# A gated linear recurrence with a convolution gate: a new order of all operations, a third x buffer, one ring for gate and gated value, a shorter setup

## The chip, the cores and the metric

The kernel runs on one core of a Trainium2 chip. Times are device microseconds. The time of a kernel is the median over its runs; one more execution is recorded by the hardware profiler, and the profile, with all its times inside the kernel, is of that one.

## What is computed

Four sequences of 6,336 tokens with 256 channels, 25,344 tokens in all, in float32. Two layers, one after the other:

```python
a_base  = sigmoid(a_param)
log_a   = 8.0 * sigmoid(r_gate) * log(clip(a_base, 1e-6, 1 - 1e-6))
a_t     = exp(log_a)
x_gated = sqrt(max(1 - a_t * a_t, 1e-6)) * sigmoid(i_gate) * x
h       = a_t[:, t] * h + x_gated[:, t]        # for every t; y[:, t] = h
...
gate    = sigmoid(sum_k conv_w[k] * y[t - 4 + k])   # causal, 5 taps
out     = (gate * (y @ w_val)) @ w_out
```

## The kernel before

**Tiling.** The tokens are cut into 27 chunks: chunk 0 has 512 tokens, chunks 1 to 23 have 1,024, chunks 24 and 25 have 512, chunk 26 has 256. From the convolution on, a chunk is worked in parts of 512 tokens. Inputs arrive with tokens on the partitions. The recurrence needs channels on the partitions (two halves, h = 0 and 1), so values are transposed by TensorE on the way.

**One operation, one name.** The whole work is a list of named operations, `name.chunk.half_or_part.bank`, in the string PLAN. The last number is the PSUM bank, or -1. The kernel goes through the list and calls `op_<name>` for each entry. Each engine takes its own operations in the order of the list, so PLAN fixes the order on every engine; waits between engines follow from what is read and written. The names, with their engine and the line of the profile:

- `ldri`, `ldx`, `ldw` (SP): loads of r and i (two DMAs, L220), of x (L224), of the two weights (L229, L231). SP issues them in order, so a load whose buffer is not free holds up those behind it.
- `tanh` (ACT, L290): tanh of half of r and i at once, in place, as bf16. Sigmoid is made of tanh.
- `srT` (PE, L295): transposes the r half, then `exp` (ACT, L304): a_t into aring. `e` (POOL, L310): its square into ering.
- `s1` (POOL, L318): 1 + tanh of i, then `u` (POOL, L345): times x, into uring. For the chunks in X_PE (0 and 1) x goes through PE into PSUM instead (`xc`, L327) and DVE does both steps (`ux`, L335, four steps for a full chunk).
- `sq` (ACT, L354): half of sqrt(1 - a squared), for up to three chunks in one entry. Sqrt is in another table of ACT than tanh and exp, so a table load (L472) stands before and after.
- `nT` (PE, L367) transposes it back, `xg` (DVE, L374) multiplies it into u, `xgT` (PE, L382) transposes the product to channels, `scan` (DVE, L395) runs the recurrence into yring.
- `conv` (PE, L407) is the 5-tap convolution by diagonal weights, `tg` (ACT, L417) its tanh into tgr, `val` (PE, L425) is y times w_val, `gv` (DVE, L430) is (1 + tanh) times val into gvr, `out` (PE, L439) is the product with w_out.
- `osbD` (DVE, L454) or `osbA` (ACT, L450) copies a part to osb, `store` writes it from ACT's queue (L459).
- `wc` (ACT, L282 and L284): casts of the weights to bf16.

**Buffers.** Rings with a fixed number of places: NRI = 3 for the r and i pair, NX = 2 for x, NA = 5 for a, NE = 5 for e, NU = 4 for u, NY = 3 for y, NOSB = 5 for outputs, NTG = 2 for the gate's tanh and NGV = 2 for the gated value. The r place of a chunk is free after its `srT`, the i place and the x place after its `u`. So the i load of chunk c waits for `u` of chunk c - 3.

**Order around the middle.** ACT works in groups of three chunks: one `sq` for three, then three `tanh`, six `exp` and six `tg`. The setup ahead of the list loads a_param and conv_w from ACT's queue, computes the scale of the exponent, and builds the diagonal weights. Loads at the head of PLAN are issued before all else.

Of the kernel before, what the change touches and what calls it, by code (L numbers as in the profile page):

```python
# [8 lines left out]
P = 128  # L9
HP = 64  # L10
# [6 lines left out]
X_PE = [0, 1]  # L17
NRI = 3
NX = 2
NA = 5  # L20
NE = 5
NU = 4
NY = 3
NOSB = 5
NTG = 2
NGV = 2
# [7 lines left out]
ldri.0.-1 ldri.1.-1 ldx.0.-1 ldx.1.-1 ldri.2.-1 ldw.-1 tanh.0.-1 srT.0.0.7 srT.0.1.5 exp.0.1.-1 exp.0.0.-1 e.0.0.-1  # L34
tanh.1.-1 e.0.1.-1 xc.0.1.0 xc.0.0.6 ux.0.0.-1 xc.1.2.1 u.0.-1 sq.0.1.-1 ux.1.2.-1 srT.1.0.0 ldri.3.-1 xc.1.1.5
ldx.2.-1 nT.0.0.7 srT.1.1.4 exp.1.0.-1 xg.0.0.-1 ux.1.1.-1 exp.1.1.-1 xc.1.0.0 tanh.2.-1 xc.1.3.5 e.1.1.-1 ux.1.0.-1
e.1.0.-1 wc.-1 srT.2.0.3 s1.2.-1 srT.2.1.2 xgT.0.0.4 exp.2.0.-1 scan.0.0.-1 exp.2.1.-1 e.2.0.-1 u.1.-1 tanh.3.-1
ldx.3.-1 ldri.4.-1 e.2.1.-1 u.2.-1 srT.3.1.3 srT.3.0.6 xgT.0.1.1 sq.1.2.-1 s1.3.-1 ldx.4.-1 ldri.5.-1 nT.2.0.7
nT.2.1.0 u.3.-1 xg.2.0.-1 exp.3.1.-1 xg.2.1.-1 nT.1.1.7 scan.0.1.-1 nT.1.0.5 tanh.4.-1 xg.1.1.-1 conv.0.0.0 xg.1.0.-1
xgT.2.0.3 e.3.1.-1 ldx.5.-1 xgT.1.1.4 ldri.6.-1 xgT.1.0.2 scan.1.1.-1 tg.0.0.-1 exp.3.0.-1 s1.4.-1 srT.4.1.1  # L40
exp.4.1.-1 scan.1.0.-1 val.0.0.4 e.3.0.-1 tanh.5.-1 srT.4.0.6 gv.0.0.-1 conv.1.0.0 u.4.-1 scan.2.0.-1 xgT.2.1.7
tg.1.0.-1 srT.5.1.5 srT.5.0.4 exp.4.0.-1 scan.2.1.-1 val.1.0.0 exp.5.1.-1 e.4.1.-1 ldx.6.-1 ldri.7.-1 exp.5.0.-1
gv.1.0.-1 conv.2.0.6 tanh.6.-1 e.5.1.-1 out.0.0.4 conv.1.1.0 osbD.0.0.-1 e.4.0.-1 val.2.0.2 tg.1.1.-1 val.1.1.4
e.5.0.-1 store.0.0.-1 tg.2.0.-1 out.1.0.0 conv.2.1.6 osbD.1.0.-1 s1.5.-1 sq.3.3.-1 gv.1.1.-1 u.5.-1 gv.2.0.-1
out.2.0.0 out.1.1.4 osbD.2.0.-1 osbD.1.1.-1 s1.6.-1 nT.3.1.3 ldri.8.-1 nT.3.0.2 ldx.7.-1 val.2.1.0 tg.2.1.-1 xg.3.0.-1
xg.3.1.-1 store.1.0.-1 u.6.-1 tanh.7.-1 gv.2.1.-1 xgT.3.1.7 nT.4.0.6 scan.3.1.-1 srT.6.0.1 srT.6.1.4 xgT.3.0.2
nT.4.1.0 nT.5.1.5 exp.6.0.-1 xg.4.0.-1 s1.7.-1 ldri.9.-1 xg.4.1.-1 exp.6.1.-1 srT.7.0.1 xg.5.1.-1 ldx.8.-1 nT.5.0.6
scan.3.0.-1 exp.7.0.-1 out.2.1.4 e.6.1.-1 tanh.8.-1 xgT.4.1.3 srT.7.1.7 xg.5.0.-1 conv.3.0.0 e.7.0.-1 osbD.2.1.-1
scan.4.1.-1 conv.3.1.4 u.7.-1 store.1.1.-1 tg.3.0.-1 xgT.4.0.6 srT.8.0.2 tg.3.1.-1 scan.4.0.-1 srT.8.1.0 exp.7.1.-1
val.3.1.4 exp.8.1.-1 gv.3.1.-1 e.6.0.-1 conv.4.1.6 ldx.9.-1 exp.8.0.-1 ldri.10.-1 xgT.5.0.3 store.2.0.-1 tg.4.1.-1  # L50
out.3.1.4 e.7.1.-1 scan.5.0.-1 tanh.9.-1 xgT.5.1.7 val.3.0.0 e.8.0.-1 conv.4.0.2 gv.3.0.-1 osbD.3.1.-1 e.8.1.-1
tg.4.0.-1 scan.5.1.-1 val.4.1.4 s1.8.-1 val.4.0.0 sq.6.3.-1 out.3.0.2 gv.4.1.-1 u.8.-1 gv.4.0.-1 osbD.3.0.-1 out.4.0.0
out.4.1.2 osbD.4.0.-1 srT.9.1.6 osbD.4.1.-1 nT.8.1.5 s1.9.-1 ldri.11.-1 nT.6.1.4 xg.8.1.-1 exp.9.1.-1 conv.5.0.2
ldx.10.-1 xg.6.1.-1 store.3.0.-1 tanh.10.-1 e.9.1.-1 nT.6.0.4 nT.7.1.1 xg.6.0.-1 nT.7.0.0 xgT.6.1.5 xg.7.0.-1 u.9.-1
xgT.6.0.4 xg.7.1.-1 srT.9.0.6 scan.6.0.-1 nT.8.0.7 exp.9.0.-1 conv.5.1.0 tg.5.0.-1 scan.6.1.-1 tg.5.1.-1 xgT.7.1.2
s1.10.-1 ldri.12.-1 store.2.1.-1 tanh.11.-1 val.5.1.0 ldx.11.-1 xg.8.0.-1 srT.10.1.3 srT.10.0.6 gv.5.1.-1 e.9.0.-1
val.5.0.4 conv.6.1.0 gv.5.0.-1 exp.10.1.-1 u.10.-1 srT.11.1.7 scan.7.1.-1 store.3.1.-1 store.4.1.-1 conv.6.0.4
tg.6.1.-1 exp.10.0.-1 srT.11.0.1 xgT.7.0.0 tg.6.0.-1 val.6.0.2 scan.7.0.-1 exp.11.0.-1 e.10.0.-1 out.5.0.4 ldri.13.-1
store.4.0.-1 ldx.12.-1 exp.11.1.-1 osbD.5.0.-1 out.5.1.0 e.10.1.-1 tanh.12.-1 conv.7.0.6 osbD.5.1.-1 e.11.0.-1
val.6.1.4 gv.6.0.-1 gv.6.1.-1 out.6.0.2 tg.7.0.-1 e.11.1.-1 store.5.1.-1 osbD.6.0.-1 xgT.8.1.6 xgT.8.0.7 s1.11.-1  # L60
out.6.1.4 scan.8.1.-1 sq.9.3.-1 val.7.0.2 u.11.-1 gv.7.0.-1 osbD.6.1.-1 conv.7.1.2 scan.8.0.-1 srT.12.0.1 srT.12.1.6
nT.9.0.0 nT.9.1.4 s1.12.-1 ldri.14.-1 nT.11.0.5 xg.9.0.-1 exp.12.0.-1 nT.10.0.7 ldx.13.-1 xg.9.1.-1 store.6.1.-1
xg.11.0.-1 store.5.0.-1 tg.7.1.-1 xgT.9.1.0 e.12.0.-1 scan.9.1.-1 exp.12.1.-1 out.7.0.2 tanh.13.-1 val.7.1.4 u.12.-1
osbD.7.0.-1 conv.8.0.0 gv.7.1.-1 nT.10.1.2 xgT.9.0.3 xg.10.1.-1 tg.8.0.-1 srT.13.0.6 scan.9.0.-1 s1.13.-1 ldri.15.-1
# [442 lines left out]
```

## Time and profile before

| | us |
|---|---|
| median of 13 runs | 309.73 (308.91 to 311.59) |
| the profiled execution | 310.86 |
| its span, first to last instruction | 309.0 |
| mean granted TensorE clock | 0.967 |
| bytes read and written | 78.39 MB and 25.95 MB |

The table sets the profiled execution beside the runs: 1.86 us of its time lie around the span, and it is 1.13 above the median. Names in the profile: PE is TensorE, PEld its weight loads, DVE VectorE, ACT ScalarE, POOL GpSimd, SP the engine that issues the loads; ACTq and SPq are the queues from which DMAs are issued. A row of a timeline has start, duration, engine, line, operation and tiles, and in square brackets how long the engine had been idle before it and what ended that. In the chain of waits, the work that ended last is followed back; its largest parts by engine are PE 26%, DMA 19%, ACT 18%, DVE 14% and "issue" 11%. No engine has a majority.

Some durations of one instruction, from the groups by form: scan of 1,024 tokens 2,340 ns, u of a full chunk 4,117, e of one half 1,895, tanh of a full chunk 3,626, gv 1,213, output copy on DVE 1,214 and on ACT 1,010, table load 1,283.

### The profile page before, as it was taken

The page shows a single profiled execution, that of the slowest core. Times are in us where ns is not written, and L with a number is a line of the kernel's source. Part 1 is how long each engine was busy: PE and PEld are TensorE (multiplying, and loading weights), DVE is VectorE, ACT ScalarE, POOL GpSimd, SP SyncE. Part 2 cuts the span into 40 slices and gives each one's busy share as a digit, 9 for nine tenths or more (in the row PEclk, how much of TensorE's full clock was granted, in tenths as well). Part 3 has the DMA queues.
Part 4 walks back from the last instruction along what each step waited for, and adds up shares of the span by engine and source line. Part 5 has one row for each costly group of instructions (what it writes and reads, how often), then busy time and mean ns, then how long its engine had stood idle before and what let it go on. Part 6 is the DMA issues. An engine that isn't in the chain of part 4 may idle for free.

```text
span 309.0 us, 6335 instructions
## 1 busy us (share of the span) xinstructions
PE 247.6 (80%) x2627; PEld 167.3 (54%) x2627; DVE 252.1 (82%) x208; ACT 278.3 (90%) x185; POOL 235.0 (76%) x118
## 2 busy tenths in 40 slices
PE   0393387958887898799499998988899988899994
PEld 0242364537555665556257664675666656565763
DVE  1052079489998989999499999999999998989993
ACT  6699999999999999998599999999999989868632
POOL 2209999997998999899996799989959993038000
PEclk9996579999999999999979999999999999999999
DMA  7999899998996999999999997999898773183555
GB/s 288 423 354 423 327 423 372 408 361 314 381 405 223 407 415 424 423 421 423 427 422 379 371 375 291 383 424 418 329 368 313 285 260 138 68 329 116 202 211 237
DMA packets 19466, 104.74 MB, mean 339 GB/s; under 512 B 2151, under 2 KB 2670, under 8 KB 10606
## 3 DMA queue, kind: packets, MB, share of 16 engines
q1 hardware_dynamic: 12224, 78.39, 64.7%
q10 hardware_dynamic: 7214, 25.96, 21.0%
q8 instruction: 20, 0.33, 0.4%
q14 instruction: 8, 0.07, 0.1%
HBM read 78.39 MB, written 25.95 MB: 338 GB/s over the span
## 4 chain that ended last, share of the span: by engine, by line
PE 26%; DMA 19%; ACT 18%; DVE 14%; issue 11%; POOL 9%; ACTq 1%; SPq 1%; DVEq 0%; POOLq 0%
DMA gate<-in_i_gate_dram 10%; DVE yring L395 8%; PE pp L407 8%; DMA xr<-in_x_dram 6%; POOL uring L345 6%; PE pp L439 5%; ACT gate L290 5%; ACT tgr L417 4%; PE pp L425 4%; ACT aring L304 4%; PE pp L367 4%; DMA out_dram<-osb 3%; DVE osb L454 3%; DVE gvr L430 3%; ACT ering L354 2%
## 5 line engine op out<-in xcount | busy, mean ns | idle before, releaser
L310 POOL TENSOR_TENSOR ering<-aring 128x1024 f32<-128x1024 f32 (+2 forms) x54 | 93.6, 1752 | 37.0 <-ACT aring L304 36.8
L395 DVE TENSOR_TENSOR_SCAN yring<-aring,yring,pp 128x1024 bf16<-128x1024 f32 (+2 forms) x52 | 113.5, 2196 | 3.7 <-PE pp L382 3.6
L345 POOL TENSOR_TENSOR uring<-gate,xr 128x2048 bf16<-128x2048 bf16 (+2 forms) x25 | 96.0, 3842 | 4.4 <-PE pp L382 2.6
L290 ACT ACTIVATE gate<-gate 128x4096 bf16<-128x4096 f32 (+2 forms) x27 | 90.2, 3340 | 8.7 <-DMA gate<-in_i_gate_dram 4.5
L407 PE MATMUL pp<-yring,diag 64*64 64x512 bf16 (+13 forms) x1224 | 65.2, 341 | 6.2 <-DVE yring L395 2.7
L430 DVE SCALAR_TENSOR_TENSOR gvr<-tgr,pp 128x1024 bf16<-128x1024 bf16 (+1 forms) x50 | 59.5, 1202 | 8.7 <-ACT tgr L417 6.7
L439 PE MATMUL pp<-wo,gvr 128*128 128x256 bf16 x396 | 52.4, 278 | 13.7 <-DVE gvr L430 8.0
L304 ACT ACTIVATE aring<-pp,khf 128x1024 f32<-128x1024 bf16 (+2 forms) x54 | 59.2, 1141 | 2.8 <-PE pp L295 2.0
L417 ACT ACTIVATE tgr<-pp 128x1024 bf16<-128x1024 f32 (+1 forms) x50 | 50.4, 1022 | 10.1 <-PE pp L407 8.6
L439 PEld LDWEIGHTS <-gvr 128*128 128x128 bf16 x396 | 42.2, 115 | 23.4 <-DVE gvr L430 11.1
L425 PE MATMUL pp<-yring,wv 128*128 128x512 bf16 (+1 forms) x200 | 50.5, 377 | 5.3 <-DVE osb L454 1.9
L454 DVE COPY osb<-pp 128x1024 f32<-128x1024 f32 x41 | 49.1, 1214 | 5.9 <-PE pp L439 5.8
L318 POOL TENSOR_SCALAR gate<-gate 128x2048 bf16<-128x2048 bf16 (+2 forms) x25 | 44.4, 1779 | 5.4 <-ACT gate L290 5.4
L407 PEld LDWEIGHTS <-diag 64*64 64x64 bf16 x1224 | 30.4, 107 | 31.7 <-issue 15.0
L354 ACT ACTIVATE ering<-ering,b 128x4096 bf16<-128x4096 f32 (+4 forms) x16 | 46.4, 2932 | 0.1
L374 DVE TENSOR_TENSOR uring<-uring,pp 128x1024 bf16<-128x1024 bf16 (+1 forms) x50 | 32.1, 673 | 12.3 <-PE pp L367 12.1
L295 PE MATMUL pp<-ident_b,gate 128*128 128x128 bf16 x396 | 31.2, 229 | 12.8 <-ACT gate L290 10.7
L295 PEld LDWEIGHTS <-gate 128*128 128x128 bf16 x396 | 26.4, 103 | 21.4 <-ACT gate L290 13.3
L367 PE MATMUL pp<-ident_f,ering 128*128 128x128 f32 x198 | 32.3, 303 | 5.5 <-ACT ering L354 3.9
L382 PE MATMUL pp<-ident_f,uring 128*128 128x128 f32 x198 | 32.0, 285 | 5.2 <-ACT tgr L417 2.8
L367 PEld LDWEIGHTS pp<-ident_f,ering 128*128 128x128 f32 x198 | 27.8, 208 | 11.7 <-ACT ering L354 4.7
L425 PEld LDWEIGHTS <-wv 128*128 128x128 bf16 x200 | 18.9, 98 | 23.2 <-issue 10.4
(33 smaller groups left out, 87.2 us busy)
## 6 DMA issues: line engine op xcount, KB each, us to landing
out_dram<-osb ACTq DMA_DIRECT2D x49, 512.0 KB, 7.4
gate<-in_r_gate_dram SPq DMA_DIRECT2D x23, 1024.0 KB, 11.5
gate<-in_i_gate_dram SPq DMA_DIRECT2D x23, 1024.0 KB, 9.9
xr<-in_x_dram SPq DMA_DIRECT2D x23, 1024.0 KB, 9.7
gate<-in_r_gate_dram SPq DMA_DIRECT2D x3, 512.0 KB, 7.6
gate<-in_i_gate_dram SPq DMA_DIRECT2D x3, 512.0 KB, 10.9
xr<-in_x_dram SPq DMA_DIRECT2D x3, 512.0 KB, 3.4
yring<-in_moe_w_val_dram SPq DMA_DIRECT2D x1, 256.0 KB
```

The lines of the kernel that those rows point to most:

```text
L290: nc.scalar.activation(out=tgate[:, s0:s0 + 2, 0:w], in_=gate[:, s0:s0 + 2, 0:w], func=ACT.Tanh, scale=0.5)
L304: nc.scalar.activation(out=dst, in_=src, func=ACT.Exp, scale=khf[:, h:h + 1], bias=khf[:, h:h + 1])
L310: nc.gpsimd.tensor_tensor(out=ering[:, c % NE, h * n:(h + 1) * n], in0=a, in1=a, op=ALU.mult)
L345: nc.gpsimd.tensor_tensor(out=u, in0=t, in1=xt, op=ALU.mult)
L367: nc.tensor.transpose(out=pp[:, d0:d0 + P], in_=src[:, w, :], identity=ident_f[:])
L395: nc.vector.tensor_tensor_scan(out=yring[:, h, y0:y0 + n], data0=aring[:, c % NA, h, 0:n], data1=src, initial=prev, op0=ALU.mult, op1=ALU.add)
L407: nc.tensor.matmul(out=pp[col * HP:(col + 1) * HP, b0 + d0:b0 + d1], lhsT=diag[r * HP:(r + 1) * HP, h, kk, :], rhs=yring[r * HP:(r + 1) * ...
L417: nc.scalar.activation(out=tgr[:, nth[k] % NTG, :, 0:n], in_=two(live["conv", k], n), func=ACT.Tanh, scale=0.5)
L425: nc.tensor.matmul(out=pp[:, (bank + m) * BANK:(bank + m) * BANK + n], lhsT=wv[:, hk, m, :], rhs=yring[:, hk, y0:y0 + n], start=(hk == 0), ...
L430: nc.vector.scalar_tensor_tensor(out=gvr[:, nth[k] % NGV, :, 0:n], in0=tgr[:, nth[k] % NTG, :, 0:n], scalar=1.0, in1=two(live["val", k], n ...
L439: nc.tensor.matmul(out=pp[:, bank * BANK + j * D:bank * BANK + (j + 1) * D], lhsT=gvr[:, nth[k] % NGV, m, 0:n].rearrange("c (p q) -> c q p ...
L454: nc.vector.tensor_copy(out=dst, in_=src)
```

## The change

PLAN is a different list: the same operations in another order on every engine. Beside it:

- `X_PE` is empty, so x of chunks 0 and 1 no longer goes through PE: six `xc` and six `ux` steps go, two `s1` and two `u` on POOL come.
- `NX` is 3 (was 2), `NU` is 3 (was 4). `gvr` is gone: `gv` writes its result over the gate's tanh in `tgr`, and `NTG` is 3 (was 2).
- Chunk 0's r and i are two loads and two tanh (`ldr`, `ldi`, `tanh.0`, `tanhi.0`).
- The setup computes log(1 + exp(-a)) in one Ln with a bias of 1 and clips after it; add, reciprocal and clip before the Ln go. Small setup tiles lie in osb's last place. The load of conv_w is issued after the first table load.
- `wc` runs on POOL.
- In the list, x loads often follow the gate loads of two or three chunks together (for instance ldri.13, ldri.14, ldri.15, then ldx.13, ldx.14, ldx.15). Twelve output copies are on ACT (were nine), all in the last chunks.

The head of the old list and of the new one, then the rest of the diff, cut:

```diff
-ldri.0.-1 ldri.1.-1 ldx.0.-1 ldx.1.-1 ldri.2.-1 ldw.-1 tanh.0.-1 srT.0.0.7 srT.0.1.5 exp.0.1.-1 exp.0.0.-1 e.0.0.-1
-tanh.1.-1 e.0.1.-1 xc.0.1.0 xc.0.0.6 ux.0.0.-1 xc.1.2.1 u.0.-1 sq.0.1.-1 ux.1.2.-1 srT.1.0.0 ldri.3.-1 xc.1.1.5
+ldr.0.-1 ldi.0.-1 ldri.1.-1 ldx.0.-1 ldw.-1 ldri.2.-1 tanh.0.-1 ldx.1.-1 tanhi.0.-1 srT.0.1.1 srT.0.0.5 exp.0.0.-1
+exp.0.1.-1 e.0.0.-1 e.0.1.-1 s1.0.-1 sq.0.1.-1 nT.0.0.1 u.0.-1 tanh.1.-1 wc.-1 xg.0.0.-1 ldri.3.-1 xgT.0.1.1 ldx.3.-1
...
-X_PE = [0, 1]
+X_PE = []
 NRI = 3
-NX = 2
+NX = 3
 NA = 5
 NE = 5
-NU = 4
+NU = 3
 NY = 3
 NOSB = 5
-NTG = 2
-NGV = 2
+NTG = 3
...
-        ap2 = const.tile([H, P], FP32, name="ap2")
-        nc.scalar.dma_start(ap2[:], a_param.rearrange("(h p) -> h p", p=P))
-        wrow = const.tile([CONV_K, D], FP32, name="wrow")
-        nc.scalar.dma_start(wrow[:], moe_conv_w[:, :])
+        ap2 = osb[0:H, NOSB - 1, 0:P]
+        nc.scalar.dma_start(ap2, a_param.rearrange("(h p) -> h p", p=P))
...
         nc.scalar.preload_act_table_set("natural_log_exp_and_others")
+        wrow = osb[0:CONV_K, NOSB - 1, D:2 * D]
+        nc.scalar.dma_start(wrow, moe_conv_w[:, :])
...
-        ksig = const.tile([P, H], FP32, name="ksig")
-        nc.vector.tensor_scalar(out=ksig[:], in0=kex[:], scalar1=1.0, scalar2=None, op0=ALU.add)
-        nc.vector.reciprocal(out=ksig[:], in_=ksig[:])
-        nc.vector.tensor_scalar(out=ksig[:], in0=ksig[:], scalar1=1e-6, scalar2=1.0 - 1e-6,
-                                op0=ALU.max, op1=ALU.min)
-        nc.scalar.activation(out=kln[:], in_=ksig[:], func=ACT.Ln)
+        kln = const.tile([P, H], FP32, name="kln")
+        nc.scalar.activation(out=kln[:], in_=kex[:], func=ACT.Ln, bias=1.0)
...
-                nc.scalar.copy(out=wv[:, hk, :, :].rearrange("p m (i c) -> p i m c", i=2),
-                               in_=wvf[:, hk, :].rearrange("p (i m c) -> p i m c", i=2, m=2))
-            nc.scalar.activation(out=wo2[:], in_=wof, func=ACT.Copy, scale=0.5)
+                nc.gpsimd.tensor_scalar(out=wv[:, hk, :, :].rearrange("p m (i c) -> p i m c", i=2),
+                                        in0=wvf[:, hk, :].rearrange("p (i m c) -> p i m c", i=2, m=2),
+                                        scalar1=1.0, scalar2=1.0, op0=ALU.mult, op1=ALU.mult)
+            nc.gpsimd.tensor_scalar(out=wo2[:], in0=wof, scalar1=0.5, scalar2=1.0, op0=ALU.mult, op1=ALU.mult)
...
+            s0, s1 = slot(c, 0), slot(c, 0) + (1 if c == 0 else 2)
+            nc.scalar.activation(out=tgate[:, s0:s1, 0:w], in_=gate[:, s0:s1, 0:w], func=ACT.Tanh, scale=0.5)
...
-            nc.vector.scalar_tensor_tensor(out=gvr[:, nth[k] % NGV, :, 0:n], in0=tgr[:, nth[k] % NTG, :, 0:n], scalar=1.0,
+            nc.vector.scalar_tensor_tensor(out=tgr[:, nth[k] % NTG, :, 0:n], in0=tgr[:, nth[k] % NTG, :, 0:n], scalar=1.0,
                                            in1=two(live["val", k], n), op0=ALU.add, op1=ALU.mult)
...
-                                     lhsT=gvr[:, nth[k] % NGV, m, 0:n].rearrange("c (p q) -> c q p", q=q)[:, j, :],
+                                     lhsT=tgr[:, nth[k] % NTG, m, 0:n].rearrange("c (p q) -> c q p", q=q)[:, j, :],
```

From the old list, the order on SP between chunks 12 and 16 is ldri.12, ldx.11, ldri.13, ldx.12, ldri.14, ldx.13, ldri.15, ldx.14, ldx.15. On ACT the new order of the group from the sqrt of chunks 9 to 11 is sq.9.3, exp.12.0, exp.12.1, tg.7.1, tanh.13, tg.8.1, tg.8.0, exp.13.1, tanh.14, exp.13.0, tg.9.0, exp.14.0, exp.14.1, tanh.15, with stores between; on POOL it is e.11.0, u.10, s1.12, u.11, e.12.1, u.12, e.12.0, e.13.1, s1.13, e.13.0, e.14.0, e.14.1, u.13.

## The prediction

> **What bounds the kernel now.** I read the busy row of the page first, then busy time by stretch, then ScalarE's timeline, then the transfer rates.
>
> ```profile
> PE 247.6 (80%) x2627; PEld 167.3 (54%) x2627; DVE 252.1 (82%) x208; ACT 278.3 (90%) x185; POOL 235.0 (76%) x118
> ```
>
> The windows view gives, for each stretch, its length and the busy time of PE, PEld, DVE, ACT and POOL, then clock, DMA share and GB/s:
>
> ```profile
> 0.00:20.00 20.00, 8.27 (x27) 4.14 (x28) 3.20 (x10) 14.10 (x12) 4.35 (x10) 1.00 0.92 362
> 20.00:100.00 80.00, 57.47 (x572) 39.62 (x571) 55.92 (x46) 79.07 (x48) 73.84 (x34) 0.89 0.93 361
> 100.00:140.00 40.00, 34.30 (x391) 23.73 (x391) 38.41 (x30) 39.90 (x24) 38.86 (x19) 1.00 1.01 418
> 140.00:150.00 10.00, 9.27 (x111) 6.03 (x109) 9.35 (x7) 5.98 (x6) 10.00 (x5) 1.00 1.02 425
> 150.00:246.15 96.15, 84.11 (x911) 58.31 (x912) 91.03 (x73) 95.74 (x58) 86.09 (x38) 0.98 0.93 367
> 246.15:309.00 62.85, 54.17 (x622) 35.47 (x620) 54.15 (x45) 43.49 (x40) 21.87 (x15) 1.00 0.52 197
> ```
>
> ACT is full from 20 to 140 and from 150 to 246. It idles in three places: 5.9 us in the first 20, 4.0 in 140:150, 19.4 in the last 62.85, where PE (54.2) and DVE (54.2) are the fuller engines. So a new order can win in the opening, in that one hole and in the tail; in between it can only lose.
>
> ACT's period for three full chunks, from start-to-start distances in its timeline (tanh 3.51, exp 1.10, gate tanh 0.91, sqrt of three chunks 5.44, table load 1.30): 3x3.51 + 6x1.10 + 6x0.91 + 5.44 + 2x1.30 = 30.6 us (154.58 to 185.30 measures 30.7). The same chunks move 3 x 4 MiB = 12.58 MB.
>
> ```profile
> GB/s 288 423 354 423 327 423 372 408 361 314 381 405 223 407 415 424 423 421 423 427 422 379 371 375 291 383 424 418 329 368 313 285 260 138 68 329 116 202 211 237
> ```
>
> No slice passes 427; a row of slices stands at 421 to 424 with loads and stores mixed, so I take 424 GB/s: 29.7 us a group, 0.9 below ACT. **Here a rule of the skill differs.** The Trainium skill, "DMA: Bandwidth & Descriptors", section "Where 436 GB/s comes from", says that between HBM and SBUF a limit of about 358 GB/s binds. By it a group would take 35.1 us, transfers would be the bound throughout, and no order could help. The row holds 424 for over 50 us, so the row decides; but transfers are only 3% from binding.
>
> **The hole.** Up to 146.8 the slices sum to 55.7 MB, 131.5 us at 424: 15.3 us of transfer time had been lost before. It came due here:
>
> ```profile
> 150.03 3.62 ACT L290 ACTIVATE gate<-gate 128x4096 bf16<-128x4096 f32 x1 [4.05 <-DMA xr<-in_x_dram]
> ```
>
> (tanh of chunk 15; its own i load was in the same queue.)
>
> **Part 1, the opening.**
>
> ```profile
> 12.14 3.62 ACT L290 ACTIVATE gate<-gate 128x4096 bf16<-128x4096 f32 x1 [1.96 <-DMA gate<-in_i_gate_dram]
> 15.77 1.28 ACT L472 ACT_TABLE_LOAD   x1
> 17.07 1.15 ACT L354 ACTIVATE ering<-ering,b 128x1024 bf16<-128x1024 f32 x1
> 18.24 1.28 ACT L472 ACT_TABLE_LOAD   x1
> 19.53 1.21 ACT L304 ACTIVATE aring<-pp,khf 128x1024 f32<-128x1024 bf16 x1
> ...
> 25.75 0.70 ACT L282 CAST wv<-yring 128x256 bf16<-128x256 f32 x2
> 26.35 0.63 ACT L284 ACTIVATE wo<-yring 128x512 bf16<-128x512 f32 x1
> ```
>
> Before, sqrt of chunk 0 and its two table loads follow tanh 1 (3.76 us); now they precede it, in the wait for the i load. Walk: three small DVE steps between Exp and Ln go (3.07 to 3.71), so the second table load ends near 4.6 instead of 5.2. The two split tanh (1.06 each, row of the 128x1024 form) run 4.6 to 6.7. The conv_w load is issued later; it took 3.2 us (1.31 to about 4.5), and PE's first srT stands behind its transposes: exp by about 8.8, POOL's squares by 10.1, sqrt and tables by 12.5. Tanh 1 starts at 12.5, not 12.1, since its loads keep their place: the setup alone wins nothing, the data hides it. Tanh 1 ends near 16.0.
>
> Then a new wait. PE's srT.1.1 stands behind xgT.0.1, which needs u.0, now on POOL (2.15 us) and needing x 0 (landed 13.3 before): u.0 15.5, xg 16.2, srT 17.0; exp of chunk 1 17.1 to 19.4, tanh 2 to 22.9, gate tanh 0 and exp of chunk 2 to 26.0, tanh 3 to 29.5, table 30.8. In the old order the same work, without that gate tanh, ends at 34.09.
>
> The weight casts leave ACT (1.3 us) and join POOL. Nearest rows: 1,024 columns at the rate of L318 (1.90 for 2,048) are 1.0 us; at the rate of L310 (1.89 for 1,024) 1.9; I take 1.2, nearer the one-input row. POOL's queue: u.0 15.5, casts 16.7, s1.1 18.6, e.1 22.3, u.1 (4.12) 26.4, e.2.1 28.3, s1.2 30.2, e.2.0 32.1. Sqrt of chunks 1 and 2 needs the last: it starts at 32.1, so ACT waits 1.3 us. Val 0, which needs the casts, comes later than they do. **The second rule** speaks against this: "GPSIMD Engine Reference", section 4.1, has two-input elementwise work about twice as slow as on VectorE. Replacing four L335 steps of 0.72 it would make u.1 5.8 us; L345 measures 4.12. By the rule POOL gives back another 1.7 us here; I keep the row. PE sheds 12 matmuls (8.7 us) and DVE six L335 steps (4.3), both in idle time, worth 0.
>
> From 32.1: sqrt to 35.8, table 37.1, then back to back to the end of the third sqrt group near 65.9, with gate tanh up to 2.1 done. Before: 69.57. **Gain 3.7.**
>
> **Part 2, the hole.** Before tanh 15 the new order has asked for r and i through 15 (31 MiB), x through 12 (12.5), weights (0.5) and 14 stores (7): 51.0 MiB, against 53.0 in the old order (one x and two stores more). That is 53.5 MB, 126.1 us at 424. Walking POOL's u times, which release the i slots, I find lost time of 2.5 at the start, 2 near 38, 2 near 42, 2 near 60 and 4 near 90: 12.3. With the 3.6 us that separate 131.1 + 15.3 from tanh 15 in the trace, the last load is in at 142.0; ACT, 3.7 early and without the hole, gets there at 142.2. So **the hole's 4.05 goes**, on a knife's edge. The third x buffer is what lets x be asked for in threes behind the gates.
>
> New waits: an i slot is free after u three chunks back. A group's three i loads are released about 4, 10 and 16 us after ACT's switch to sqrt; the first is needed at 11.1, and takes 2.5 us plus 2 of landing, so a backlog over 2.5 us stalls ACT. I charge **2.5 us** in all (bounds: nothing; and 1.8 a group over six groups, 11). NU=3 makes u.c wait for xgT of c-3: xgT precedes or closely follows the srT whose square is ahead of u on POOL, except u.18 and u.21, which also stand behind tanh 19 and 22; their i loads still have about 2 us: 0, or up to 1 each. The gate tanh of a part now waits for the out matmuls three parts back (in place gv); in nine cases those follow the conv on PE by one to four groups of 0.9 to 1.2 us, and ACT has other work queued only behind it: between 0 and 1 us each, most hidden by DVE's lag; inside the 2.5. Small tiles laid in osb's last buffer cost 0: its first output comes four parts later.
>
> **Part 3, the tail.** From the table load before the sqrt of chunks 21 and 22 (246.15) to the end are 62.85 us, with PE 54.17 busy. At that point the new order has val.18.1, val.19.0, conv.19.0 and out.18.1 behind it: 0.87 + 0.87 + 1.20 + 0.87 by the chain's distances, less one srT (0.2): 3.6 us. DVE also sheds three gv (3.4) and three output copies (3.6), which go to ACT with its 19 idle us. **Gain 3.6.** ACT reaches the point with two gate tanh more (1.8) and two half exp less (1.5): **cost 0.3**.
>
> **Sum.** 309.0 - 3.7 - 4.05 + 2.5 - 3.6 + 0.3 = 300.5 us of span. The profiled execution took 310.86, 1.86 around its span; it lies 1.13 above the median of 309.73. So 302.4 in such an execution, **301.2** at the median.
>
> **Rivals.**
> - *The gains of the opening and the hole are hidden by transfers* (0.20): they stay the limiter at 140, only the tail wins 3.6: 306. For it: 0.9 us of slack a group. Against: 2 MiB less asked for by then.
> - *Released too late, slower* (0.15): POOL carries 10.4 us more (u.0 2.15, u.1 4.12, s1 2.95, casts 1.2), its u release the i slots, and all three loads of a group come in a burst behind x. With the first i load 2.5 us over its margin in each of six groups: 300.5 - 2.5 + 15 = 313, 313.7 at the median. It turns slower from 1.8 us a group. Against: POOL has 0.5 to 1 us a chunk in hand.
> - *Better* (0.10): no new waits, and the 2 us of further PE idle at 246:262 close: 296.7.
> - *The forecast* (0.55), own range 297.5 to 304.5.
>
> Changes within 0.3% (about 0.9 us) can't be told from none. Faster: 0.55 + 0.10 + most of 0.20 = 0.81; same 0.05; slower 0.14. Range 294.5 to 311: below for the better case, above for the start of the late-release case.
>
> **What would show it.** Tanh 1 near 12.5 with sqrt 0 before it; sqrt of chunk 1 waiting on POOL near 31 to 32; sqrt 3 to 5 ended near 65; no ACT gap over 2 us between 70 and 235; sqrt of 21 about 241 and 59 us from there. Wrong if tanh waits for the i load in several groups, or if PE idles in the tail.

## The result, and the profile after

| | before | after |
|---|---|---|
| median, us | 310.07 (308.85 to 312.44, 48 runs) | 314.98 (312.70 to 317.79, 11 runs) |
| ratio, 95% interval | | 1.015 (1.0128 to 1.0173) |
| span of the profiled execution | 309.0 | 313.1 |

The change makes the kernel 1.5% slower by the ratio, 4.9 us by the medians. The ratio leaves out the two slowest of the 11 runs (317.74 and 317.79), whose time was over 1.5% above the fastest. The forecast was 301.2, the range ended at 311. The busy row and the transfer rates of the page of after:

```profile
PE 248.5 (79%) x2615; PEld 169.7 (54%) x2615; DVE 246.3 (79%) x197; ACT 280.7 (90%) x186; POOL 245.4 (78%) x125
...
GB/s 291 401 426 428 374 367 422 201 350 406 430 270 282 356 412 409 340 372 421 418 268 350 382 420 428 340 406 425 324 346 347 378 174 279 251 110 204 67 308 197
```

The totals hardly tell anything: ACT is busy 2.4 us longer, POOL 10.4, DVE 5.8 less. The rates do: the row of six slices at 421 to 427 that the kernel before has between about 116 and 162 us is broken up; dips to 270, 340, 268, 340 come back every four to five slices, 31 to 39 us, about the period of a group of three chunks.

**Where the time went.** Cut at the forecast's own places (the end of the table load behind the sqrt of chunks 3 to 5, and the start of the one ahead of the sqrt of 21 and 22). In the kernel before, gate tanh 2.1 comes behind the first of these table loads; 69.57 is its end, so that both kernels have done the same work on ACT at this cut.

| | before | after | difference | forecast |
|---|---|---|---|---|
| opening | 69.57 | 67.59 | -2.0 | -3.7 |
| middle | 176.58 | 187.18 | +10.6 | -1.25 |
| tail | 62.85 | 58.33 | -4.5 | -3.6 |
| span | 309.0 | 313.1 | +4.1 | -8.5 |

The forecast's middle is the hole's -4.05, the waits' +2.5 and +0.3 of added work. So the opening paid half, the tail a little more than forecast, and the middle has the whole miss. The view of waits of ACT for the middle of after (what waited, for what; us in total, times, longest) and then the same view of before:

```profile
ACT aring L315 <- DMA gate<-in_i_gate_dram: 3.5, 2, 2.3
ACT gate L296 <- DMA gate<-in_i_gate_dram: 3.1, 2, 2.2
ACT tgr L428 <- DMA gate<-in_r_gate_dram: 1.9, 1, 1.9
ACT tgr L428 <- PE pp L418: 1.5, 3, 0.8
ACT tgr L428 <- PE pp L450: 0.9, 1, 0.9
ACT aring L315 <- DMA gate<-in_r_gate_dram: 0.7, 1, 0.7
ACT aring L315 <- PE pp L450: 0.7, 1, 0.7
ACT gate L296 <- ACT tgr L428: 0.5, 1, 0.5
```

```profile
ACT gate L290 <- DMA xr<-in_x_dram: 4.0, 1, 4.0
```

Before there is one wait, the hole. After, it is replaced by six waits for transfers, 9.2 us, and by waits for PE and the rings, 3.8 us with a last row of 0.2. The remaining 1.7 of the 10.6 us is not more work: ACT has 104 instructions in the middle of both kernels (two gate tanh more are set off by two half exp fewer), and their durations add up to 181.2 us after and 181.6 before. What differs is how far they overlap: an ACT instruction that follows at once starts about 0.1 us before the one ahead of it has ended, one that had to wait does not. The overlaps add up to 9.6 us before and 7.5 after, so ACT is busy 172.0 us there before and 173.7 after. 5.2 + 3.8 + 1.7 = 10.7. That the additional waits are what cost the overlap is likely; no run tests it.

Three of these rows are odd: exp (L315) and gate tanh (L428) read neither an r nor an i load. ACT's timeline of after tells why:

```profile
113.42 1.24 ACT L315 ACTIVATE aring<-pp,khf 128x1024 f32<-128x1024 bf16 x1
115.43 0.34 ACTq L470 DMA_DIRECT2D out_dram<-osb  x1
115.81 1.21 ACT L315 ACTIVATE aring<-pp,khf 128x1024 f32<-128x1024 bf16 x1 [1.15 <-DMA gate<-in_i_gate_dram]
```

A store stands between the two exp in ACT's queue, and it is the store that waits. The traces of both kernels show that all 136 loads and stores take turns at eight completion semaphores, 17 on each, in a fixed order. A DMA is held on its queue until the transfer eight before it in that turn has landed: this store left at 115.43, and the i load of chunk 12, eight before it, had landed at 115.41. A store so waits for a load that it has nothing to do with, and ACT stands behind the store. Stores held in this way make 6.1 of the 9.2 us, tanh's waits for their own i loads 3.1. The same pair of rows is in the kernel before, at the hole:

```profile
144.94 1.04 ACT L417 ACTIVATE tgr<-pp 128x1024 bf16<-128x1024 f32 x1
149.57 0.34 ACTq L459 DMA_DIRECT2D out_dram<-osb  x1
```

The store of chunk 8, part 0, left at 149.57, and tanh 15 began at 150.03. The load in its turn is that of x 14. The two loads on SP's queue, with their landing times, i of chunk 15 first and then x of chunk 14:

```profile
135.96 0.33 SPq L220 DMA_DIRECT2D gate<-in_i_gate_dram  x1
DMA to landing us min/median/max: 9.8/9.8/9.8
```

```profile
136.38 0.43 SPq L224 DMA_DIRECT2D xr<-in_x_dram  x1
DMA to landing us min/median/max: 13.1/13.1/13.1
```

So i 15 had landed at 145.80 (r 15 at 142.36), before ACT became free for tanh 15 at 145.98. X 14 landed at 149.49, just ahead of the store. The forecast took this for tanh 15's wait for its own i load.

### The profile page after: what moved, and what is told of

It is laid out like the page before. It is cut to its first block, busy times and chain, and to the rows that moved or that the text cites. A ratio compares the mean times of both kernels' runs of the same rounds, so it can differ in the third digit from the quotient of the medians.

```text
span 313.1 us, 6316 instructions
## 1 busy us (share of the span) xinstructions
PE 248.5 (79%) x2615; PEld 169.7 (54%) x2615; DVE 246.3 (79%) x197; ACT 280.7 (90%) x186; POOL 245.4 (78%) x125
## 4 chain that ended last, share of the span: by engine, by line
POOL 23%; DMA 20%; ACT 18%; PE 17%; issue 13%; DVE 7%; SPq 0%; ACTq 0%; POOLq 0%; DVEq 0%
POOL uring L356 13%; DMA gate<-in_i_gate_dram 8%; DMA xr<-in_x_dram 7%; PE pp L418 5%; ACT ering L365 5%; POOL ering L321 5%; POOL gate L329 5%; DMA gate<-in_r_gate_dram 5%; PE pp L450 4%; ACT gate L296 4%; ACT tgr L428 4%; DVE yring L406 3%; PE pp L378 3%; ACT aring L315 2%; DVE tgr L441 2%
## 5 line engine op out<-in xcount | busy, mean ns | idle before, releaser
L356 POOL TENSOR_TENSOR uring<-gate,xr 128x2048 bf16<-128x2048 bf16 (+2 forms) x27 | 102.2, 3789 | 8.7 <-PE pp L393 5.8
L418 PE MATMUL pp<-yring,diag 64*64 64x512 bf16 (+12 forms) x1224 | 67.8, 353 | 6.7 <-DVE yring L406 5.8
L441 DVE SCALAR_TENSOR_TENSOR tgr<-tgr,pp 128x1024 bf16<-128x1024 bf16 (+1 forms) x50 | 59.0, 1202 | 15.2 <-PE pp L436 8.6
L315 ACT ACTIVATE aring<-pp,khf 128x1024 f32<-128x1024 bf16 (+2 forms) x54 | 59.4, 1134 | 6.8 <-DMA gate<-in_i_gate_dram 3.5
L428 ACT ACTIVATE tgr<-pp 128x1024 bf16<-128x1024 f32 (+1 forms) x50 | 49.9, 1018 | 12.2 <-PE pp L418 9.3
L465 DVE COPY osb<-pp 128x1024 f32<-128x1024 f32 x38 | 45.3, 1216 | 15.2 <-PE pp L450 12.3
L450 PE MATMUL pp<-wo,tgr 128*128 128x256 bf16 x396 | 51.7, 277 | 6.5 <-DVE tgr L441 5.0
L329 POOL TENSOR_SCALAR gate<-gate 128x2048 bf16<-128x2048 bf16 (+2 forms) x27 | 47.3, 1757 | 5.3 <-ACT gate L296 5.3
L418 PEld LDWEIGHTS <-diag 64*64 64x64 bf16 x1224 | 33.1, 110 | 31.9 <-issue 16.8
L450 PEld LDWEIGHTS <-tgr 128*128 128x128 bf16 x396 | 41.9, 115 | 15.5 <-issue 8.2
L385 DVE TENSOR_TENSOR uring<-uring,pp 128x1024 bf16<-128x1024 bf16 (+1 forms) x50 | 32.1, 676 | 20.1 <-PE pp L378 9.9
L378 PE MATMUL pp<-ident_f,ering 128*128 128x128 f32 x198 | 34.0, 319 | 16.5 <-ACT ering L365 11.7
L306 PE MATMUL pp<-ident_b,gate 128*128 128x128 bf16 x396 | 32.6, 233 | 14.7 <-ACT gate L296 14.3
```

The costliest lines, as they stand in the source:

```text
L315: nc.scalar.activation(out=dst, in_=src, func=ACT.Exp, scale=khf[:, h:h + 1], bias=khf[:, h:h + 1])
L329: nc.gpsimd.tensor_scalar(out=t, in0=t, scalar1=1.0, scalar2=1.0, op0=ALU.add, op1=ALU.mult)
L356: nc.gpsimd.tensor_tensor(out=u, in0=t, in1=xt, op=ALU.mult)
L378: nc.tensor.transpose(out=pp[:, d0:d0 + P], in_=src[:, w, :], identity=ident_f[:])
L418: nc.tensor.matmul(out=pp[col * HP:(col + 1) * HP, b0 + d0:b0 + d1], lhsT=diag[r * HP:(r + 1) * HP, h, kk, :], rhs=yring[r * HP:(r + 1) * ...
L428: nc.scalar.activation(out=tgr[:, nth[k] % NTG, :, 0:n], in_=two(live["conv", k], n), func=ACT.Tanh, scale=0.5)
```

## The experiments

Theories after the result: **stores hold ACT**; **i loads are asked for too late**, because u on GpSimd frees their place too late (the forecast's slower rival); **the rings** of three make waits; **the transfers have no room**, whatever asks for them.

Each row below is the median, the ratio to before, and ACT's waits in the middle of the profiled execution, for transfers and for all else (0.2 us or more, between the table loads behind the sqrt of chunks 3 to 5 and of 21 and 22). A wait counts as one for transfers when the profile names a DMA as what ended it. It also counts as one when it ended with the landing of tanh's own load, or of the load in the turn of the store just ahead, though the profile names an engine; this moves waits between the columns in b_head, a_stores, a_tiny, a_sp, a_rf, a_u and b_ulate.

| run | median | ratio (95%) | transfers | else |
|---|---|---|---|---|
| before | 310.07 | 1 | 4.0 | 0 |
| after | 314.98 | 1.015 (1.0128 to 1.0173) | 9.2 | 3.8 |
| b_hole | 307.70 | 0.9932 (0.9912 to 0.9952) | 2.2 | 0 |
| b_hole2 | 306.83 | 0.9875 (0.9848 to 0.9902) | 0 | 1.2 |
| b_tiny | 308.27 | 0.9945 (0.9925 to 0.9965) | 2.4 | 0 |
| b_head | 311.37 | 1.0036 (1.0014 to 1.0058) | 4.2 | 0.2 |
| b_both | 307.68 | 0.9912 (0.9887 to 0.9936) | 0 | 0.3 |
| a_stores | 321.18 | 1.0385 (1.0341 to 1.0429) | 11.9 | 7.9 |
| a_tiny | 317.14 | 1.0239 (1.0202 to 1.0276) | 10.5 | 3.5 |
| a_sp | 319.86 | 1.0302 (1.0251 to 1.0354) | 7.1 | 9.7 |
| a_rf | 321.75 | 1.0372 (1.0337 to 1.0408) | 17.0 | 3.4 |
| a_ntg4 | 316.51 | 1.0216 (1.0187 to 1.0246) | 10.2 | 5.9 |
| a_s1 | 311.87 | 1.0053 (1.0023 to 1.0082) | 5.3 | 5.4 |
| a_u | 315.92 | 1.0194 (1.0156 to 1.0231) | 8.4 | 4.9 |
| b_ulate | 337.42 | 1.0902 (1.0876 to 1.0927) | 27.6 | 2.1 |
| a_half | 306.23 | 0.9862 (0.9825 to 0.9899) | 0.8 | 4.5 |
| b_half | 304.66 | 0.9826 (0.9802 to 0.9849) | 0 | 0 |
| a_q | 304.29 | 0.9786 (0.9742 to 0.9829) | 0.5 | 3.2 |
| b_q | 303.61 | 0.9779 (0.9751 to 0.9808) | 0 | 0 |

Names with b_ start from the kernel before, those with a_ from the changed one. For b_hole, b_hole2, b_tiny and b_head, a difference in us is against the runs of before made together with them (medians of 310.02 to 310.50). In b_head the 4.2 is the hole again: the profile names a copy on DVE there, but it is the same place (4.17 us ahead of tanh 15, at 150.13), and the store ahead of it left just after x 14 had landed at 149.59.

### The hole in the kernel before

**b_hole** moves one store behind tanh 15 and the gate tanh after it:

```diff
-... e.13.0.-1 store.8.0.-1 tanh.15.-1 gv.8.1.-1 ... osbD.8.1.-1 tg.9.1.-1 e.13.1.-1
+... e.13.0.-1 tanh.15.-1 gv.8.1.-1 ... osbD.8.1.-1 tg.9.1.-1 store.8.0.-1 e.13.1.-1
```

> The kernel before, with one store (chunk 8, part 0) issued from ScalarE's queue after tanh 15 instead of ahead of it; nothing else. Theory 'stores hold ScalarE' (a store waits in ScalarE's in-order queue until an earlier, unrelated load has landed, since all transfers take turns at a small number of completion semaphores): the 4.05 us hole ahead of tanh 15 closes, time falls by 3 to 4 us, ratio about 0.988. Theory of the prediction ('transfers were behind and tanh 15 waited for its own gate loads'): tanh 15 waits as long as before, change within 1 us.

It won 2.4 us. Tanh 15 no longer waits, at 144.23. But another wait has appeared further on:

```profile
147.85 3.13 ACTq L459 DMA_DIRECT2D out_dram<-osb  x2
151.01 1.28 ACT L472 ACT_TABLE_LOAD   x1 [2.25 <-DMA xr<-in_x_dram]
```

The moved store left at 147.85, while ACT was still at work. It is the next one, store 8.1, whose turn is now behind the load of x 15: that landed at 150.57, the store left at 150.64, and the table load behind it had stood for 2.25 us. So neither theory's number was met, and the place of the wait already speaks for the stores. **b_hole2** puts the store behind the sqrt; by this both store 8.0 and store 8.1 take their turn behind old stores (of chunks 6 and 7):

```diff
-... s1.14.-1 sq.12.3.-1 scan.11.0.-1
+... s1.14.-1 sq.12.3.-1 store.8.0.-1 scan.11.0.-1
```

> The kernel before with one store (chunk 8, part 0) issued from ScalarE's queue behind the sqrt of chunks 12 to 14; nothing else. It then waits for a store long landed. Theory 'that store, not tanh 15's loads, made the hole': with no wait left in its place the whole 4.05 us go, 305.5 to 306.5 (ratio 0.986 to 0.989). Theory 'the transfers are late there whatever waits': no better than with the store behind gate tanh 9 (307.7).

The ratio of 0.9875 is in the expected band, the median of 306.83 is 0.3 us above it. ACT's timeline of b_hole2 at the place of the hole:

```profile
144.90 1.06 ACT L417 ACTIVATE tgr<-pp 128x1024 bf16<-128x1024 f32 x1
145.80 3.67 ACT L290 ACTIVATE gate<-gate 128x4096 bf16<-128x4096 f32 x1
```

Tanh 15 follows at once, 4.2 us earlier than before, with the order of the loads unchanged. The hole was the store's, all of it; of its 4.05 us the kernel keeps 3.7 by the medians, and 1.2 us of other waits stand in the middle. **b_tiny** moves nothing and shifts only the turn:

```diff
+        def op_tiny():
+            nc.sync.dma_start(tiny[:], xf[0:1, 0:8])
...
         def op_ldx(k, bank):
             c = k[0]
+            if c in (11, 13, 14, 19):
+                op_tiny()
```

> The kernel before with six loads of 32 bytes added on SyncE's queue (ahead of the r load of 12, the x loads of 11, 13, 14 and 19, the r load of chunk 12 and the i load of 16), so that stores 8.0, 8.1 and their neighbours take their turn at the completion semaphores behind stores long landed; every order is kept. Theory 'stores hold ScalarE': the 4.05 us hole goes without anything being moved, 3 to 4.5 us faster than before (305.5 to 307). Theory of the prediction ('tanh 15 waits for its own late loads'): the hole stays, within 1 us of before, or slower by the added loads.

Six loads more, 1.75 us less: the hole is gone, and a wait of 2.36 us is left at 141.60, where the shifted turn holds another store. About half of what was expected, in the direction that only the store theory has.

### The same cure in the changed kernel

**a_stores** moves five stores, for instance:

```diff
-... tg.17.0.-1 ... store.15.0.-1 store.14.1.-1 store.15.1.-1 store.14.0.-1 tg.17.1.-1 val.17.0.2 tanh.23.-1
+... tg.17.0.-1 ... store.15.0.-1 store.14.1.-1 tg.17.1.-1 val.17.0.2 tanh.23.-1 store.15.1.-1 store.14.0.-1
```

> The changed kernel, with five stores (4.0, 11.1, 13.1, 14.0, 15.1) issued from ScalarE's queue a little later, each behind the ScalarE work that it stood ahead of while waiting; nothing else. Theory 'stores hold ScalarE': the gaps of ScalarE near 116, 206, 214 and 241 us (1.15 + 2.31 + 0.74 + 1.85 = 6.05 us) close and the time falls by 4 to 6 us against the changed kernel, to about 309.5 (ratio to before about 0.998). Theories 'gate loads are asked for too late by GpSimd' and 'the transfer rate itself limits': the waits come back at the next tanh, gain 0 to 2 us (313 to 315).

A miss for all: 6 us slower than the changed kernel. The stores freed their output places later, and DVE's copies and PE's out matmuls stood behind them (in one place ACT waited 3.14 us for the output copy of a store that stood next in its queue). Tanh still waited for i loads, and store 11.1 now waits 0.80 us for x 20. **a_tiny** adds three small loads, so that stores 4.0, 11.1 and 17.1 wait for old stores:

> The changed kernel with three loads of 32 bytes added on SyncE's queue (ahead of the r load of chunk 13, the x load of 20, the i load of 25), so that the turn at the completion semaphores shifts by one and stores 4.0, 11.1 and 17.1 wait for stores that have long landed, not for loads just asked for; every order is kept. Theory 'stores hold ScalarE': the gaps at 115.8 and 206.5 (1.15 + 2.31 us) go and 2 to 4 us are gained against the changed kernel (311 to 313). Theory 'whatever frees ScalarE there runs into loads that are late anyway': the wait reappears at the next tanh, 0 to 1 us gained (314 to 315).

A miss for all again, 2 us lost: six tanh wait for their i loads, 0.6 to 2.1 us each, and store 13.1 waits 2.1 us for r 21. **a_sp** issues the stores from SP (`nc.scalar.dma_start` in `op_store` becomes `nc.sync.dma_start`):

> The changed kernel with its stores issued from SyncE's queue, between the loads, instead of from ScalarE's; nothing else. Theory 'stores hold ScalarE': ScalarE's gaps near 116, 206, 214 and 241 us (6 us together) go, and the time falls by 3 to 6 us against the changed kernel (309 to 312), unless a store that waits for its output holds the loads behind it on SyncE's queue. Theory 'gate loads are asked for too late by GpSimd': tanh waits as before and somewhat longer, 315 to 320.

It is 4.9 us slower than the changed kernel, in the band of late requests. The stores' 6.1 us on ACT go, but tanh's waits for their own loads rise from 3.1 to 7.1, so waits for transfers fall only to 7.1. And 7.42 us come in one place, for a convolution: it stood on PE behind an output copy that waited 6.91 us on DVE for a store to free its place, and the load of r 13 left SP only at 122.99, behind such stores. Stores hold ACT here too, but freeing it in these three ways gains nothing: what comes next is late as well.

### Late requests

How long ahead of its tanh is an i load issued? From the timelines of SP and ACT, chunks 7 to 23: 14.2 us on average before, 9.2 after; for the first chunk of each group 18.3 and 8.2. An i load takes 9.9 (before) and 8.2 us (after) to land by the median. So the changed kernel asks about one landing time ahead, with nothing to spare. The row of SP's waits in after:

```profile
SPq L218 <- POOL uring L356: 172.8, 23, 16.0
```

Here u of the middle chunk of a group stands behind the group's squares, where before it stood ahead of them. **a_s1** shortens POOL by letting `s1` work on `CHUNKS[c] * H // 16` columns:

> The changed kernel with GpSimd's addition of 1 to the tanh of the input gate done on one sixteenth of the columns of each chunk only, so it leaves out the rest: about 1.7 us of GpSimd less per chunk, so that the loads of the input gate are asked for earlier. Theory 'gate loads are asked for too late by GpSimd': most waits of tanh and of the stores for landing loads go, 8 us less than the changed kernel or better (307 or lower). Theory 'transfers have no room, wherever they are asked for from': 0 to 4 us less (311 to 315).

3.1 us less: within what the "no room" theory allowed, and not what late requests alone would give. Work is left out here, so part of the gain may be POOL's own. **a_rf** asks for the r loads as soon as their place is free, not behind waiting i loads:

```diff
-... ldri.13.-1 srT.12.0.6 ... u.11.-1 ... ldri.14.-1
+... ldr.14.-1 ... ldi.13.-1 srT.12.0.6 ... ldr.15.-1 ... u.11.-1 ... ldi.14.-1
```

> The changed kernel with the r loads of chunks 6 to 26 taken out of their pairs and asked for as soon as PE has read the r slot, ahead of i loads that wait for GpSimd; nothing else. Theory 'SyncE's queue stands at an i load that waits for GpSimd's u while the transfers run dry': the dry stretches (slices of 201, 270, 282 GB/s) fill, 3 to 7 us less than the changed kernel (308 to 312). Theory 'the transfers are as full as they can be': no change or a loss, since i loads land later behind the r loads (314 to 318).

6.8 us slower, beyond the band of either theory. The r loads took the transfers' time ahead of the i loads that ACT needed first: r 21 had landed at 216.20, and tanh 21 waited 5.93 us for its i load, which landed at 223.59. Waits for transfers rise to 17.0 us; asking earlier for more bytes does not help by itself. **a_u** undoes the move of u (in five groups), **b_ulate** makes it in the kernel before. One group of a_u's edit:

```diff
-... e.10.1.-1 s1.11.-1 e.11.1.-1 ... e.10.0.-1 ... s1.10.-1 e.11.0.-1 ... u.10.-1 ... sq.9.3.-1 ... ldri.13.-1
+... e.10.1.-1 s1.10.-1 u.10.-1 ldri.13.-1 ... s1.11.-1 e.11.1.-1 ... e.10.0.-1 e.11.0.-1 ... sq.9.3.-1
```

> The changed kernel with, in five groups, the +1 and u of the middle chunk (7, 10, 13, 16, 19) moved on GpSimd's queue ahead of the group's last squares, as the kernel before has them, and the loads that this frees (and the x that it needs) asked for as much earlier. In the kernel before the i load of the first chunk of a group is asked for 18.3 us ahead of its tanh on average, in the changed one 8.2 us. Theory 'the i load of each group's first chunk is asked for too late': the waits of tanh and of stores in the middle go and 5 to 9 us are gained against the changed kernel (306 to 310). Theory 'the rate, or the rings, hold it wherever the loads are asked for': 0 to 2 us gained (313 to 315).

> The kernel before with only this of the change: in five groups u of the middle chunk (7, 10, 13, 16, 19) moved on GpSimd's queue behind the group's squares, and with it the loads that it frees. Theory 'the i load of each group's first chunk is asked for too late': tanh of chunks 10, 13, 16, 19, 22 waits for its i load or stores do, 5 to 10 us slower than before (315 to 320). Theory 'the loss came with the new rings or the rest of the order': within 2 us of before (308 to 312).

A pair that doesn't agree. Made alone in the kernel before, the move costs 27 us, far beyond what was expected: 27.6 us of waits for transfers. Undone in the changed kernel, it lengthens the lead to 12.0 us (15.2 for the first of a group), but the waits for transfers fall only from 9.2 to 8.4 (those of tanh for its own load even rise, from 3.1 to 5.3), the others rise from 3.8 to 4.9, and the time stays. So a late request can cost this kernel a great deal, and it is still not the one cause in the changed order.

### The rings

**a_ntg4** has `NTG = 4`; to find room, the bf16 identity is read as a strided view of the fp32 one. That changes values, not work.

> The changed kernel with a fourth buffer in the ring that holds gate tanh and gated value (room for it: the bf16 identity is read as a strided view of the fp32 one, two tiny setup tiles lie in a buffer that is free then). Theory 'the ring of three makes gate tanh wait for the out matmuls three parts back': the gaps at 91.34, 171.59 and part of others close, 1.5 to 3 us less than the changed kernel (312 to 313.5). Theories 'stores hold ScalarE' and 'gate loads asked for too late': the small gain is lost at the next wait for a transfer, 0 to 1 us less (314 to 315).

The wait for out matmuls three parts back (0.9) is gone, the time is no better. **b_rings** (337.12 us, ratio 1.0862, 1.0816 to 1.0909) is the kernel before with `NX = 3`, `NU = 3` and the one ring of three:

> The kernel before, its order of work and its setup unchanged, with only the buffers of the change: three x buffers, three u buffers, gate tanh and gated value in one ring of three, the small setup tiles in the last output buffer. Theory 'the new rings cost waits of their own' (gate tanh waits for out matmuls three parts back, u waits for a scan's transposes three chunks back): 3 to 8 us slower than before (313 to 318). Theory 'the loss comes from the new order and from what it makes the transfers' queues wait for': within 1.5 us of before (309 to 311.5).

It tells nothing of the rings by themselves: in the old order three gate tanh and thirteen u are listed ahead of the last reader of the place that they now share. So out of parts 3.0, 5.0 and 22.0 and the products of thirteen chunks read overwritten values, and the waits turn round with them. A ring of four u in the changed kernel had no room and wasn't tried.

### Fewer bytes

**a_half** and **b_half** store `[:, 0:n // P // 2, :]` of each part, **a_q** and **b_q** `[:, 0:1, :]`.

> The changed kernel that writes only half of each part's output rows, so 13 MB of 105 MB are left out; all waits and queues stay. Theory 'the transfer rate limits': loads land earlier by up to 1.2 us a store pair, ScalarE's gaps behind transfers close, 8 to 12 us less than the changed kernel (303 to 307). Theory 'the loads are asked for too late, the rate has room': 0 to 3 us less (312 to 315).

> The kernel before that writes only half of each part's output rows, so 13 MB of 105 MB are left out; all waits and queues stay. Theory 'the new order is worse fed than the old one at the same bytes': the kernel before wins only its hole, 3 to 5 us (305 to 307), and the difference between the two kernels closes to 0 or turns round (the changed one took 306.2). Theory 'both are bound by the rate alike': the kernel before wins 8 to 10 us (300 to 302).

> The changed kernel that writes only a quarter of each part's output rows (an eighth of the bytes more are left out than with half of them). Theory 'only the transfers stand between this order and the forecast': 301 to 303. Theory 'new waits for PE and DVE, which ScalarE has at half the writes too (4.5 us), and its own added work stay': 304.5 to 306.5, no better than at half.

> The kernel before that writes only a quarter of each part's output rows. With half of them ScalarE waits nowhere in the middle any more, so both theories say: no further gain, 304 to 305; a further fall would show a cost of the stores beside ScalarE's waits.

With half the writes both kernels lose nearly all their waits for transfers; the changed one gains 8.7 us, as the rate theory has it, the other 5.4, a little more than its hole. ACT's waits in the middle of a_half, the first four rows (b_half's view is empty):

```profile
ACT tgr L428 <- PE pp L436: 1.3, 1, 1.3
ACT tgr L428 <- PE pp L418: 1.3, 3, 0.6
ACT aring L315 <- PE pp L306: 0.9, 1, 0.9
ACT gate L296 <- DMA gate<-in_i_gate_dram: 0.8, 1, 0.8
```

At a quarter they take 304.29 (301.47 to 305.40) and 303.61 (303.12 to 304.32): no difference to be told. So with hardly any wait for transfers left the new order is no faster: its middle is 5.2 us longer there too (184.8 against 179.6, between the cuts of the first table). Of these, 3.7 are waits, most of them for PE, and 1.4 are less overlap on ACT (9.0 against 10.4 us; the durations add up to the same). That eats the 1.0 and 4.4 us of opening and tail.

### The opening

**b_head** makes only the opening's part of the change in the kernel before (setup, casts on POOL, tanh 0 split, tanh 1 behind the first sqrt), **b_both** has the hole closed as well.

```diff
-... tanh.0.-1 srT.0.0.7 ... e.0.0.-1 tanh.1.-1 e.0.1.-1 ... sq.0.1.-1 ux.1.2.-1
+... tanh.0.-1 tanhi.0.-1 srT.0.0.7 ... e.0.0.-1 e.0.1.-1 ... sq.0.1.-1 tanh.1.-1 ux.1.2.-1
```

> The kernel before with only the opening's part of the change: shorter setup, weight casts on GpSimd, tanh of chunk 0 split in two, tanh 1 after the first sqrt; x still added on TensorE for chunks 0 and 1, rings as before. Theory 'the opening was sized rightly, and the changed kernel lost it by its u work on GpSimd': the table load after sqrt 3 to 5 ends 2.5 to 4 us earlier than in the kernel before (69.57) and the time falls by as much (306 to 307.5). Rival 'the opening is worth only the 2 us that the changed kernel shows, or its gain is taken back at the hole ahead of tanh 15': time within 1.5 us of before, and the hole grows by what the opening won.

> The kernel before with both its own-sized gains: the opening's part of the change (as in the run that had it alone) and the store of chunk 8, part 0, behind the sqrt of chunks 12 to 14. Theory 'the opening's gain is ScalarE's and only the hole had swallowed it': it adds to the 3.7 us that the store's move won alone, 304.5 to 305.5. Theory 'the transfers of the first 50 us take the opening's gain back at tanh 5': no better than the store's move alone, 306 to 308.

The table load behind the second sqrt ends at 37.18 in b_head, 1.9 us earlier than before (39.10). Then tanh 5 waits 1.79 us for its i load at 46.80, and by the third sqrt 0.3 is left. The rival's time is met (b_head is 1.2 us slower than before), but not its place: the hole grew only from 4.05 to 4.17, and the gain had gone at tanh 5. What makes the 1.2 us is not shown. With the hole closed (b_both) it is the same: 1.99 us at tanh 5, and no gain over b_hole2.

## Why the prediction was wrong, by its own steps

**The step that failed** is the term "I charge 2.5 us in all" for new waits. It measured 13.0: 9.2 for transfers and 3.8 for PE and the rings. The span came out 12.6 us above the forecast's (313.1 against 300.5). Of these, 10.5 are this term, 1.7 are missing from the opening, 1.4 are the overlap lost on ACT (1.7, where the forecast charged 0.3), and the tail gave back 0.9 more than forecast; the sum is right to 0.1. The terms one by one:

**"Transfers are only 3% from binding."** This is where the charge was made too small. 424 GB/s was read from the best 46 us of the profile (six slices of 421 to 427; the forecast says over 50 us) and then used for all stretches. Two rows of 4 us of after, and the same stretches of before (columns as in the forecast's windows):

```profile
128.00:132.00 4.00, 4.00 (x55) 3.43 (x53) 3.50 (x5) 3.97 (x3) 4.00 (x2) 1.00 0.88 295
156.00:160.00 4.00, 3.45 (x30) 2.60 (x28) 3.96 (x5) 3.99 (x2) 3.26 (x3) 1.00 0.67 229
```

```profile
128.00:132.00 4.00, 3.07 (x24) 2.42 (x24) 4.00 (x5) 3.99 (x5) 3.03 (x4) 1.00 1.02 420
156.00:160.00 4.00, 3.38 (x16) 2.28 (x16) 4.00 (x3) 4.00 (x1) 3.92 (x3) 0.67 1.03 425
```

Fewer loads in flight go with a lower rate. Counted from issue to landing in stretches of 2 us between 40 and 240 us of both traces, the rate is 286 GB/s on average with fewer than two loads in flight, 373 with two to three, 406 with more. The scatter is wide (188 to 430 in after with 2 to 2.5 loads in flight), so this is a tendency and no rule. An order that runs ahead finds its places full and its queue thin; that the thin queue is what lowers the rate is argued, and the one run that asked for loads earlier to fill it (a_rf) got slower. Added up over such rows from 100 to 164 us, after lost 7.5 us of transfer time at 424, before 0.5. The forecast weighed the Trainium skill's 358 GB/s ("DMA: Bandwidth & Descriptors", "Where 436 GB/s comes from") against this row and dropped it. For a kernel on one core that was right: the same page's section "Bandwidth" gives about 358 GB/s for each of two cores that stream together and measures 425 for one core alone, and the rows of 420 to 425 agree with the latter. But what the 358 would have led to, that the transfers bind and an order wins little, was nearer to the runs.

**"So the hole's 4.05 goes."** Two errors. The reading: it was a store in ACT's queue, and the row ahead of the one quoted showed it; tanh 15's own loads had landed (b_hole2 took 3.7 us off by one moved token). The sum: 12.3 us of transfer time lost ahead of tanh 15. It was more, not less, than the 15.3 of before. The window of after up to tanh 15:

```profile
0.00:149.90 149.90, 106.45 (x1063) 73.12 (x1063) 100.49 (x82) 138.53 (x85) 131.90 (x71) 0.92 0.93 367
```

367 GB/s over 149.9 us is 55.0 MB, 129.7 us at 424: 20.2 lost. Tanh 15 began at 149.9, as late as before, not at 142.2; its i load landed at 148.84, not at 142.0.

**"I charge 2.5 us in all" for new waits** (bounds 0 and 11; measured 13.0). The landing time in it was too small: 2.5 + 2 us were taken for an i load, the median from issue to landing was 8.2, with a lead of 8.2 us for the first chunk of a group. The margin after the switch to sqrt was then used up. And the stores' share (6.1 of the 9.2) was not in the sum at all. The waits for PE and the rings were to hide inside the 2.5; they are 3.8, and 3.2 to 4.5 with fewer bytes as well.

**The opening, 3.7.** Tanh 1 at 11.92 (forecast 12.5) and the sqrt of chunks 1 and 2 at 31.36 (32.1) were right, with a wait for POOL of 0.53 instead of 1.3:

```profile
11.92 3.62 ACT L296 ACTIVATE gate<-gate 128x4096 bf16<-128x4096 f32 x1
...
31.36 3.71 ACT L365 ACTIVATE ering<-ering,b 128x4096 bf16<-128x4096 f32 x1 [0.53 <-POOL ering L321]
```

"Then back to back" was not: 0.56 us for an i load at 44.93 and 1.35 for a convolution at 49.89, in a stretch where the granted TensorE clock was 0.50 (46.9 to 50.1). The gain was 2.0, and b_head and b_both show that even the old order loses such a gain again to a load.

**The tail, 3.6.** Right: 58.33 us against the forecast's 59.

**The rivals.** "Gains hidden by transfers" (306) had the right resource, for the opening as for the hole, but stopped at no loss. "Released too late, slower" (313.7) had the size, and b_ulate shows its mechanism at full price; but tanh's own waits are only 3.1 of the 13.0 us, and a_u shows that undoing the release doesn't bring the time back.

**What stays open:** what makes the 3.8 us of waits for PE, and why each single change to the new order moves a wait instead of removing it. One rival for the first was not tested, the granted TensorE clock. In the middle of after it was halved twice, from about 81 to 88 us and from 163 to 166; the first stretch, clock in the third column from the end:

```profile
81.00:87.70 6.70, 6.03 (x41) 3.09 (x42) 2.49 (x2) 6.55 (x7) 4.45 (x3) 0.50 1.03 428
```

Three of the waits (0.93 at 91.34, 0.77 at 169.83, 0.74 at 171.59, together 2.4 of the 3.8) come within 6 us of these stretches. The kernel before has one such stretch (155 to 159) and no wait behind it, and a_q has waits for PE at full clock too (1.46 us the longest), so the clock can be a part of it at most. No variant of the changed kernel with all its bytes and work has a median below its 314.98.

**A version that beats both** is the kernel before with its one store moved (b_hole2): 306.83 us, 2.6% below the changed kernel (306.83/314.98 = 0.974).

## What to carry to other kernels

When an engine waits in its timeline, read the queue row just ahead of it: a DMA issued from that engine's queue may be what waits, and moving one token can be worth more than a new order. A peak transfer rate read from the best stretch need not hold in an order that asks for its loads differently; size a plan by the rate at which its buffers come free, and take a load's landing time from the trace, not from its bytes. Two resources within a few per cent of each other leave little for work taken off one of them: test with fewer bytes what the order would win if the other were free.

## What had not been expected of the hardware

- Six loads of 32 bytes made a kernel faster by 1.75 us (b_tiny, 0.9945), by shifting which transfer a store waits for.
- The DMA engines can be nearly full by their busy share and still move a quarter less: 295 GB/s at a share of 0.88 (128 to 132 us of after), and 318 GB/s at 1.04 (160 to 164), against 420 at 1.02.
- One step on GpSimd, moved in five groups, cost 27 us (b_ulate): single tanh waited 4.66, 5.66 and 6.98 us for their i loads.
